# Moving four stores, two weight passes and four sums in a fused attention and MLP kernel

## The chip, the cores and the metric

The kernel runs on one core of a Trainium2 chip. The metric is device time in microseconds (us). The kernel before takes 871.37 us, the median of three runs (870.72, 871.37 and 871.62).

Engines are named as in the profile: PE multiplies matrices (PEld is its loading of weights), DVE is the vector engine, ACT the scalar engine, POOL the third one for element work. SP computes nothing: it issues DMAs, in the order of its queue. ACT and POOL issue some DMAs as well.

## What is computed

Two blocks stand behind each other. The first is attention with a mask: a query sees a key only if six sign bits of their projections agree.

```python
q_bits = (np.einsum('bhsd,dk->bhsk', q, proj) > 0)      # 4 batches, 8 heads, 768 rows, 64 columns
k_bits = (np.einsum('bhsd,dk->bhsk', k, proj) > 0)
...
mask = q_bucket[:, :, :, None] == k_bucket[:, :, None, :]
scores = np.where(mask, scale * np.matmul(q, k.transpose(0, 1, 3, 2)), -1000000000.0)
attn = softmax(scores)
attn_out = np.matmul(attn, v)
```

The second is an MLP on the heads put side by side, `x` of 3072 rows and 512 columns:

```python
h = x @ w_in                                            # 512 x 2048
g = np.maximum(h, 0.0) + alpha * np.minimum(h, 0.0)
out = g @ w_out                                         # 2048 x 512
```

All of it is float32.

## The kernel before

**Attention** (lines 1190 to 1256) is a loop over 16 pairs of heads, `pi`. For each pair PE makes twelve cells of scores (L782, six blocks of keys by two halves of the queries; the key block is the outer index). A cell lies in one of three buffers of PSUM, which the hash of the next pair (L732) and the totals of a pair (L828) use as well, in turn; ACT takes the exponential of the cell (L785) and sets the buffer free. Then PE hashes the next pair (L732), multiplies the exponentials with `v` (`attend`, L815) and sums them (`totals`, L828). DVE adds the exponentials up for the totals (`add_first` L793 to `add_total` L804), turns the totals out of PSUM (L842), and from them makes the factors that the result is multiplied with (L843 to L860). POOL copies pieces of these factors between partitions in four small copies (L851, L852), which the turn at L854 waits for. The result `x` of a pair is stored to the scratch tensor `x_s` in memory by SP (L861).

The sign bits of the next pair come out of ACT as the tile `hr` (L736) and go to the tiles `kb` and `qb` by eight small DMAs (L743): two by ACT's queue, six by POOL's. Each covers one head and one half of the columns. The first cell needs half 0 of `kb` and `qb`, the second needs half 1 of `qb`; half 1 of `kb` is first needed by the seventh.

**Preparing the weights** lies beside attention. `w_in` and `w_out` come as 32 pieces, two for each pair (numbers `i` = 2 `pi` and `i` + 1), loaded by POOL's queue (L590). A piece passes ACT twice (`weight_abs`, L604 and L608) and DVE four times (L614, L620, L645, L648). `weight_abs(i + 2)` and `weight_abs(i + 3)` stand at the end of pair `pi`, ahead of the next pair's exponentials. Four pieces of `w_in` make a group in the tile `wsi`; POOL adds four sums to it (`one`, L667), one each time that `weight_sums` is called, that is, twice a pair. When the four are done, the fifth entry of the list `sums_due` is the function `store`: four DMAs by SP to the scratch tensor `w_in_s` (L672), 448 KB each. The four groups' stores are called in pairs 5, 8, 12 and 15; the last of them in `divide(14)`, which stands in pair 15. `w_out` is stored to `w_out_r` without sums (L659).

**The MLP** multiplies with a scheme of seven products for eight blocks. It runs after the loop, over 60 steps: in each of the 4 batches eight steps `ff1` with `w_in` (`f_0` to `f_7`) and seven steps `ff2` (`z`). A step `f_n` needs the tile `wi` number n, 896 KB, loaded from `w_in_s` by SP (`load_w`, L891). There are three such buffers. Numbers 0, 1 and 2 are loaded in pairs 9, 11 and 15, the rest as buffers come free. It also needs differences of `x`: the blocks are loaded from `x_s` (`load_x`, L875) in pair 5 (block 0 of a list of four), pair 6 (blocks 2 and 3) and pair 8 (block 1), and `sum_x` (L885) makes four differences on DVE, whole tiles of 128 x 768, in pairs 8, 10, 12 and 14. Block 3 becomes the tile `x5`, block 0 `x0`; the first difference is `x5 - x0`. From L1010 on, POOL loads pieces of `w_out_r` (`wo`) beside the first steps of the MLP, 512 KB each.

**What sets the order.** The framework schedules each engine's queue by itself, except where an instruction goes through `do`: that pins it behind the instruction that the program wrote last for the same engine, pinned or not. All work of PE, DVE, ACT and POOL in the loop is pinned so. On SP the loads of `q`, `k` and `v` and the stores are not pinned; the loads of `x` for the first batch and the first three of `wi` are (`pinned`, L866). What a queue holds is issued in order: an instruction that waits holds back all behind it. At the end of a pair the program writes for SP: `v` of pair `pi + 2`, then `load_w` and `load_x`, then `q` and `k` of pair `pi + 3`, in four DMAs each.

```python
        if pi + 2 < NPAIR:
            load(pi + 2, "v")
        if pi in (9, 11, 15):
            load_w((9, 11, 15).index(pi))
        if pi in (5, 6, 8):
            load_x(0, *{5: (0,), 6: (2, 3), 8: (1,)}[pi])
```

Of the kernel before, what the change touches and what calls it, by code (L numbers as in the profile page):

```python
# [13 lines left out]
ALU = mybir.AluOpType  # L14
# [393 lines left out]
def fast_path(  # L408
# [12 lines left out]
    nc = tc.nc  # L421
    P = 128
    B, H, S, D = q.shape
# [62 lines left out]
    def load(pi, name):  # L486
        b, hp = pairs[pi]
        src = {"q": q, "k": k, "v": v}[name]
        if name == "v":
            t = pool.tile([P, 2, NC * D], F32, name=f"vn{pi}", tag="vn")  # L490
            nc.sync.dma_start(t, src[b, 2 * hp : 2 * hp + 2].rearrange("h (p c) d -> p h (c d)", c=NC))
            nat[name, pi] = t
        elif pi and name in BY_BLOCKS:
            load_blocks(pi, name)
        else:
            load_part(pi, name, slice(0, NC), nc.sync)
# [102 lines left out]
    def weight_abs(i, engine=None):  # L599
        i = order[i]  # L600
        lo, hi = halves(i)
        wx[i] = pool.tile([P, 512], F32, name=f"wx{i}", tag="wx")
        wr[i] = pool.tile([P, 512], I32, name=f"wr{i}", tag="wr")
        do(ACT.activation(wr[i], lo, AF.Copy, scale=2.0 ** -29))  # L604
        if engine is DVE:
            do(DVE.tensor_scalar(wx[i].bitcast(U32), hi, 0x7FFFFFFF, None, op0=ALU.bitwise_and))
            return
        do(ACT.activation(wx[i], hi.bitcast(F32), AF.Abs))  # L608
# [39 lines left out]
        do(DVE.tensor_tensor(dst.bitcast(I32), x, r, op=ALU.add))  # L648
        return (dst if i < HW else dst[:, 0])[:, :1]

    sums_due = []

    def weight_group(i):

        i = order[i]
        if i >= HW:
            n, m = divmod(i - HW, 2)
            if m == 1:
                nc.sync.dma_start(w_out_r[:, :, n].rearrange("m p d -> p m d"), wst[HW + n])  # L659
            return  # L660
        n, m = divmod(i, 4)
        if m < 3:
            return
        w = wst[n]

        def one(to, a, op, c):
            do(POOL.tensor_tensor(w[:, to], w[:, a], w[:, c], op=op))  # L667

        def store():
            c, kk = divmod(n, 2)  # L670
            for ii in range(4):
                nc.sync.dma_start(w_in_s[4 * c + ii][:, :, kk], w[:, :, ii])  # L672


        for x in ((3, 5, 2), (5, 0, 5), (4, 3, 0), (6, 1, 4)):
            sums_due.append((one, (x[0], x[1], ALU.subtract, x[2])))
        sums_due.append((store, ()))

    late_sum = const.tile([P, 1], F32, name="late_sum")

# [45 lines left out]
    def hash_bits(pi):  # L726

        ps = two_banks(f"hs{pi}")[:, 0, :CW]
        for half in range(2):
            for n, name in enumerate("kq"):  # L730
                c = D * n + 32 * half
                do(PE.matmul(  # L732
                    ps[c : c + 32], wh2, tr[name, pi][:, half * CW : (half + 1) * CW], start=True, stop=True,
                ))
        raw = pool.tile([P, CW], BF16, name=f"hr{pi}", tag="hr", bufs=1)
        do(ACT.activation(raw, ps, AF.Sign, bias=hb2))  # L736
        bits["q", pi], bits["k", pi] = qbs[pi % 2], kb
        for half in range(2):
            for n, name in enumerate("kq"):
                for s in range(2):  # L740
                    c = D * n + 32 * half + NB * s
                    queue = nc.gpsimd if half or name == "q" else nc.scalar
                    queue.dma_start(  # L743
                        bits[name, pi][D * s : D * s + 2 * NB, half * CW : (half + 1) * CW], raw[c : c + 2 * NB],
                    )

    def hash_first(half):

# [25 lines left out]
    def scores(pi, cells):  # L774
        for kc, g in cells:
            sc = two_banks(f"sc{pi}_{kc}_{g}")
            ks = slice(kc * P, (kc + 1) * P)
            qs = slice(g * CW, (g + 1) * CW)
            for what, first in ((bits, True), (tr, False)):
                for s in range(2):  # L780
                    r = slice(D * s, D * s + D)
                    do(PE.matmul(  # L782
                        sc[:, s, :CW], what["k", pi][r, ks], what["q", pi][r, qs], start=first, stop=not first,
                    ))
            do(ACT.activation(pts[kc][:, g, :, :CW], sc[:, :, :CW], AF.Exp, scale=SCALE / DOWN))  # L785
# [46 lines left out]
    def divide(pi, between=lambda: None):  # L832

        b, hp = pairs[pi]
        n = CW // 32
        a = pool.tile([P, CW], F32, name=f"st{pi}", tag="st", bufs=1)
        r = pool.tile([P, n], F32, name=f"rc{pi}", tag="rc")
        rr = pool.tile([P, NCH, n], F32, name=f"rr{pi}", tag="rr")  # L840
        d = pool.tile([P, NCH, CW], F32, name=f"dn{pi}", tag="dn", bufs=1)
        do(DVE.transpose(a, sums[pi][:, 0, :CW]))  # L842
        do(DVE.tensor_scalar(r, a.rearrange("p (n w) -> p n w", w=32)[:, :, 0], S * EPS, None, op0=ALU.add))  # L843
        for g in range(NCH):
            do(DVE.reciprocal(rr[:, g], r))
        vsum[pi] = pool.tile([P, 1], F32, name=f"vs{pi}", tag="vs")
        do(DVE.tensor_scalar(vsum[pi], av[pi][:, 0, CW : CW + 1], EPS, None, op0=ALU.mult))
        weight_sums(1, vsum[pi])
        for q0 in (0, D):
            q1 = q0 + 32  # L850
            do(POOL.tensor_copy(rr[q0 : q0 + 32, 1], rr[q1 : q1 + 32, 1]))  # L851
            do(POOL.tensor_copy(rr[q1 : q1 + 32, 0], rr[q0 : q0 + 32, 0]))  # L852
        between()
        do(DVE.transpose(  # L854
            d.rearrange("p g w -> p (g w)"),
            rr.rearrange("p g n -> p (g n)").unsqueeze(2).to_broadcast([P, NCH * n, 32]),
        ))

        x = mid.tile([P, NCH, CW], F32, name=f"x{pi}", tag="x", bufs=1)
        do(DVE.scalar_tensor_tensor(x, av[pi][:, :, :CW], vsum[pi], d, op0=ALU.add, op1=ALU.mult))  # L860
        nc.sync.dma_start(x_s[b, hp], x.rearrange("p g w -> p (g w)"))  # L861
# [15 lines left out]
            ))  # L877
            x_m[b, m] = t

    def sum_x(b, n, engine):  # L880

        to, a, c = ((3, 5, 0), (5, 2, 5), (4, 2, 3), (6, 4, 1))[n]
        if to != 5:
            x_m[b, to] = mid.tile([P, 2, CW], F32, name=f"x{b}_{to}", tag=f"x{to}", bufs=1)
        do(engine.tensor_tensor(x_m[b, to], x_m[b, a], x_m[b, c], op=ALU.subtract))  # L885

    def load_w(n):

# [301 lines left out]
    for pi in range(NPAIR):  # L1190
        i = 2 * pi

        def weight_begin():
            if pi == 1:
                turn_blocks(2, "q")
            if pi + 1 < NPAIR:
                turn_blocks(pi + 1, "k")
            weight_clamp(i)
            weight_parts(i)
            add_first(pi)  # L1200

        if pi:
            scores(pi, CELLS)
            divide(pi - 1, weight_begin)
        else:
            rest = [c for c in CELLS if c not in ahead]
            scores(pi, rest[:4])
            weight_abs(0, DVE)
            scores(pi, rest[4:])
            add_first(pi)  # L1210
            weight_clamp(0)
            weight_parts(0)
        if pi in (8, 10, 12, 14):
            sum_x(0, (8, 10, 12, 14).index(pi), DVE)
        weight_sum(i)
        weight_group(i)
        load_weight(i + 3)
        if pi == 0:
            weight_abs(1, DVE)
        weight_clamp(i + 1)  # L1220
        add_third(pi)
        add_last(pi)
        add_total(pi)
        weight_parts(i + 1)
        weight_sums(1, weight_sum(i + 1))
        weight_group(i + 1)
        load_weight(i + 4)
        if pi + 1 < NPAIR:
            hash_bits(pi + 1)
            do(ACT.activation(tr["q", pi + 1], tr["q", pi + 1], AF.Copy, scale=DOWN))  # L1230
        if 0 < pi < NPAIR - 2:
            turn_blocks(pi + 2, "q")
        attend(pi)
        if pi + 1 == NPAIR:
            now = ff1(0, 0)
            now.step(1)
        totals(pi)
        if pi + 1 == NPAIR:
            now.step(5)
            divide(pi)  # L1240
        else:
            weight_abs(i + 2)
        if pi + 2 < NPAIR:
            load(pi + 2, "v")
        if pi in (9, 11, 15):
            load_w((9, 11, 15).index(pi))
        if pi in (5, 6, 8):
            load_x(0, *{5: (0,), 6: (2, 3), 8: (1,)}[pi])
        if pi == 1:
            setup_alpha()  # L1250
        for name in "qk":
            magnitude(pi, name)
            if pi + 3 < NPAIR:
                load(pi + 3, name)
        if pi + 1 < NPAIR:
            weight_abs(i + 3)


# [95 lines left out]
```

## Time and profile before

| | |
|---|---|
| median of three runs | 871.37 us |
| profiled execution | 872.62 us |
| its span, first to last instruction | 870.8 us |
| PE busy | 860.5 us (99%) |
| DVE, ACT, POOL busy | 734.2, 375.0, 119.1 us |
| granted clock of PE, mean | 0.998 |
| memory read, written | 104.87, 28.31 MB |
| first cell of pair 1, of pair 15 | 29.0, 297.6 us |
| first product of the MLP, end of its last | 315.8, 864.1 us |

The profile is that of one execution. Its page gives busy times of the engines, the costliest groups of instructions and the DMAs. Other views of the same trace give the waits (who waited for whom), the instructions in order of time, and the busy time, granted clock and memory traffic of any stretch. In the timeline a row is start, duration, engine, line, operation, output<-input, and in brackets the idle time of the engine ahead of it and what ended it. Rows of SP are the issues of DMAs, not their transfers: how long the data takes is read from the traffic of a stretch.

### The profile page before, as it was taken

To read this page: it belongs to the slowest core of one execution; us is meant where nothing else is said; L and a number is where in the kernel's file an instruction comes from. 1 tells how busy PE (TensorE), PEld (TensorE's weight loads), DVE (VectorE), ACT (ScalarE), POOL (GpSimd) and SP (SyncE) were. 2 spreads that over 40 slices of the span, in tenths; PEclk is the share of its full clock that TensorE was granted. 3 is DMA by queue.
4 is the path that set the end of the run, shared out by engine and by line. 5 is a ranking of instruction groups with operands and counts; after the bars stand their busy time and mean duration, and the time that the engine had idled before them with its cause. 6 is when DMAs were issued, how large, how long until landed. Compare 5 with 4: busy or idle time off the path is not lost.

```text
span 870.8 us, 14641 instructions
## 1 busy us (share of the span) xinstructions
PE 860.5 (99%) x5458; PEld 575.5 (66%) x5458; DVE 734.2 (84%) x1188; ACT 375.0 (43%) x682; POOL 119.1 (14%) x253
## 2 busy tenths in 40 slices
PE   9999999999999999999999999999999999999996
PEld 4444444444445445569985559996558997557996
DVE  6999989999999987899887669897659898568886
ACT  6787878868778733331113331112332112332111
POOL 1322423333435310210000000000000000000001
PEclk9999999999999999999999999999999999999999
DMA  8956796998697446785334335333425433420242
GB/s 197 188 135 130 185 248 176 184 228 207 130 259 177 144 132 236 257 285 222 115 115 121 133 126 165 121 145 92 166 95 163 145 109 115 164 84 1 97 151 72
DMA packets 171104, 135.35 MB, mean 155 GB/s; under 512 B 126240, under 2 KB 155088, under 8 KB 167440
## 3 DMA queue, kind: packets, MB, share of 16 engines
q1 hardware_dynamic: 158528, 108.44, 44.2%
q0 software_dynamic: 9488, 24.56, 9.3%
q10 hardware_dynamic: 3008, 1.33, 0.6%
q8 instruction: 45, 0.74, 0.3%
q14 instruction: 35, 0.29, 0.1%
HBM read 104.87 MB, written 28.31 MB: 153 GB/s over the span
## 4 chain that ended last, share of the span: by engine, by line


## 5 line engine op out<-in xcount | busy, mean ns | idle before, releaser
L782 PE MATMUL sc<-qT,kT 64*128 64x384 f32 x768 | 155.7, 483 | 0.0
L785 ACT ACTIVATE pt<-sc 128x768 f32<-128x768 f32 x192 | 151.5, 811 | 1.2 <-PE sc L782 1.2
L815 PE MATMUL av<-pt,vn 128*32 128x385 f32 (+1 forms) x1536 | 127.0, 485 | 0.0
L815 PEld LDWEIGHTS av<-pt,vn 128*32 128x32 f32 x1536 | 50.3, 109 | 73.8 <-issue 69.8
L782 PEld LDWEIGHTS sc<-qT,kT 64*128 64x128 f32 x768 | 69.2, 187 | 35.0 <-issue 34.0
L975 DVE TENSOR_TENSOR g<-g,g 128x384 f32<-128x384 f32 x128 | 68.3, 554 | 2.2
L1094 POOL DMA_DIRECT2D out_dram<-o x4 | 2.2, 555 | 474.3 <-DVE o L1087 474.3
L782 PE MATMUL sc<-qb,kb 64*128 64x384 bf16 x384 | 65.3, 323 | 1.4 <-ACT pt L785 0.7
L971 DVE SCALAR_TENSOR_TENSOR g<-h,alpha 128x384 f32<-128x384 f32 x60 | 36.8, 614 | 25.2 <-ACT h L964 25.1
L1032 DVE TENSOR_TENSOR ws<-wl 128x512 f32<-128x512 f32 x56 | 38.4, 686 | 21.9 <-DMA wl<-w_out_s 18.0
L1040 DVE TENSOR_TENSOR gs<-g,gs 128x768 f32<-128x768 f32 x56 | 53.3, 952 | 1.0
L1040 DVE TENSOR_TENSOR gs<-g 128x768 f32<-128x768 f32 x56 | 53.2, 950 | 0.0
L782 PEld LDWEIGHTS <-kb 64*128 64x128 bf16 x384 | 21.8, 94 | 36.9 <-issue 13.2
L604 ACT ACTIVATE wr<-raw 128x512 int32<-128x512 uint32 x32 | 22.1, 691 | 35.9 <-DVE wsi L648 18.4
L793 DVE TENSOR_TENSOR accp<-pt,pt 128x1536 f32<-128x1536 f32 x16 | 28.1, 1759 | 8.4 <-ACT pt L785 8.4
L743 POOL DMA_DIRECT2D qb<-hr x60 | 30.1, 507 | 22.8 <-ACT hr L736 22.8
L798 DVE TENSOR_TENSOR accd<-accd,pt 128x1536 f32<-128x1536 f32 x16 | 28.1, 1759 | 1.7
L804 DVE TENSOR_TENSOR accd<-accd,accp 128x1536 f32<-128x1536 f32 x16 | 28.1, 1758 | 0.6
L801 DVE TENSOR_TENSOR accp<-accp,pt 128x1536 f32<-128x1536 f32 x16 | 28.0, 1753 | 0.0
L797 DVE TENSOR_TENSOR accd<-pt,pt 128x1536 f32<-128x1536 f32 x16 | 28.0, 1750 | 0.0
L1230 ACT ACTIVATE qT<-qT 128x768 f32<-128x768 f32 x15 | 12.7, 844 | 26.5 <-DMA kb<-hr 16.4
L915 PE MATMUL f_0a<-x,wi 128*128 128x384 f32 x64 | 23.5, 490 | 0.0
(366 smaller groups left out, 1767.7 us busy)
## 6 DMA issues: line engine op xcount, KB each, us to landing
wi<-w_in_s SPq DMA_DIRECT2D x32, 896.0 KB
wl<-w_out_s SPq DMA_DIRECT2D x16, 1024.0 KB
wl<-w_out_r SPq DMA_DIRECT2D x12, 1024.0 KB
raw<-in_moe_w_in_dram POOLq DMA_DIRECT2D x15, 512.0 KB, 5.2
raw<-in_moe_w_out_dram POOLq DMA_DIRECT2D x14, 512.0 KB, 4.9
w_in_s<-wsi SPq DMA_DIRECT2D x16, 448.0 KB
qn<-in_q_dram SPq DMA_DIRECT2D x64, 96.0 KB
vn<-in_v_dram SPq DMA_DIRECT2D x16, 384.0 KB
```

The costliest lines, as they stand in the source:

```text
L743: queue.dma_start(bits[name, pi][D * s : D * s + 2 * NB, half * CW : (half + 1) * CW], raw[c : c + 2 * NB],)
L782: do(PE.matmul(sc[:, s, :CW], what["k", pi][r, ks], what["q", pi][r, qs], start=first, stop=not first,))
L785: do(ACT.activation(pts[kc][:, g, :, :CW], sc[:, :, :CW], AF.Exp, scale=SCALE / DOWN))
L793: do(DVE.tensor_tensor(accp[pi], p(0), p(1), op=ALU.add))
L797: do(DVE.tensor_tensor(accd[pi], p(3), p(4), op=ALU.add))
L798: do(DVE.tensor_tensor(accd[pi], accd[pi], p(5), op=ALU.add))
L804: do(DVE.tensor_tensor(accd[pi], accd[pi], accp[pi], op=ALU.add))
L815: do(PE.matmul(av[pi][D * s + t : D * s + t + 32, g, :w], nat["v", pi][:, s, kc * D + t : kc * D + t + 32], pts[kc][:, g, s, :w], start=(k ...
L971: do(DVE.scalar_tensor_tensor(new_g(b, m)[:, i], h, al, h, op0=ALU.mult, op1=ALU.max))
L975: do(DVE.tensor_tensor(new_g(b, to)[:, i], g_m[b, x][:, i], g_m[b, y][:, i], op=ALU.subtract))
L1032: do(DVE.tensor_tensor(t, w2[b, n, x], w2[b, n, y], op=op))
L1040: do(DVE.tensor_tensor(t, g2[b, n, x], g2[b, n, y], op=ALU.subtract))
```

## The change

Five things are changed.

- The load of `v` is pinned in SP's queue (for pairs from 2 on), and the stores of `w_in`'s groups are pinned too. They are no longer written where `weight_sums` comes to them: that only puts them on the list `stores_due`, and they are written at the end of the pair, behind the load of `v` and ahead of `load_w`, `load_x` and the loads of `q` and `k`. In pair 15 there is no load of `v` any more; what the program wrote last for SP there is the store of pair 15's `x` (L861, in `divide(15)`).
- `sum_x` makes one half of a difference (128 x 384) in each of the pairs 7 to 14, in place of a whole one in every second pair.
- `weight_abs(3)`, which stood at the end of pair 0, stands behind the first three cells of pair 1.
- POOL issues the bits of `q`'s half 1 ahead of those of `k`'s half 1.
- `weight_abs(i + 3)` at the end of a pair is left out in pair 0 accordingly.

```diff
-            nc.sync.dma_start(t, src[b, 2 * hp : 2 * hp + 2].rearrange("h (p c) d -> p h (c d)", c=NC))
+            ins = nc.sync.dma_start(t, src[b, 2 * hp : 2 * hp + 2].rearrange("h (p c) d -> p h (c d)", c=NC))
+            if pi > 1:
+                do(ins)
...
-    sums_due = []
+    sums_due, stores_due = [], []
...
             for ii in range(4):
-                nc.sync.dma_start(w_in_s[4 * c + ii][:, :, kk], w[:, :, ii])
+                do(nc.sync.dma_start(w_in_s[4 * c + ii][:, :, kk], w[:, :, ii]))
...
-        sums_due.append((store, ()))
+        sums_due.append((stores_due.append, (store,)))
...
-        for half in range(2):
-            for n, name in enumerate("kq"):
-                for s in range(2):
-                    c = D * n + 32 * half + NB * s
-                    queue = nc.gpsimd if half or name == "q" else nc.scalar
+        for name, half, queue in (("k", 0, nc.scalar), ("q", 0, nc.gpsimd), ("q", 1, nc.gpsimd), ("k", 1, nc.gpsimd)):
+            for s in range(2):
+                c = D * "kq".index(name) + 32 * half + NB * s
...
-    def sum_x(b, n, engine):
+    def sum_x(b, n, engine, k=slice(0, 2)):
...
-        do(engine.tensor_tensor(x_m[b, to], x_m[b, a], x_m[b, c], op=ALU.subtract))
+        do(engine.tensor_tensor(x_m[b, to][:, k], x_m[b, a][:, k], x_m[b, c][:, k], op=ALU.subtract))
...
-        if pi:
+        if pi == 1:
+            scores(1, CELLS[:3])
+            weight_abs(3)
+            scores(1, CELLS[3:])
+            divide(0, weight_begin)
+        elif pi:
...
-        if pi in (8, 10, 12, 14):
-            sum_x(0, (8, 10, 12, 14).index(pi), DVE)
+        if 7 <= pi < 15:
+            kk = (pi - 7) % 2
+            sum_x(0, (pi - 7) // 2, DVE, slice(kk, kk + 1))
...
             load(pi + 2, "v")
+        while stores_due:
+            stores_due.pop(0)()
         if pi in (9, 11, 15):
...
-        if pi + 1 < NPAIR:
+        if 0 < pi < NPAIR - 1:
             weight_abs(i + 3)
```

## The prediction

> **What bounds the kernel now.** I read the page's busy times first, then PE's own waits, then the instructions in order of time around each place that the change touches, and last the traffic of short stretches.
>
> ```profile
> PE 860.5 (99%) x5458; PEld 575.5 (66%) x5458; DVE 734.2 (84%) x1188; ACT 375.0 (43%) x682; POOL 119.1 (14%) x253
> ```
>
> PE is the bound from end to end: 870.8 - 860.5 leaves 10.3 us, and most of that is the first and last few. So nothing can be won but PE's stalls, and whatever makes PE wait is lost in full. The view of PE's waits shows little:
>
> ```profile
> PE z_4a L915 <- DMA wl<-w_out_r: 0.9, 1, 0.9
> PE sc L782 <- ACT pt L785: 0.7, 2, 0.4
> PE sc L782 <- DVE st L842: 0.4, 2, 0.2
> ```
>
> Ends of matmuls are modelled, so I measured stalls by starts. An undisturbed pair takes 18.98 us from first cell to first cell, its cells 0.807 us each. Starts later than that, by the trace's start times: pair 1's fourth cell 0.54; pair 6's first three 0.61 in all; pair 9's third 0.60, 11's 0.38, 13's 0.38; around pair 14's totals 0.15, and 0.46 in pair 15. Sum 3.1 us: 0.54 for the weight passes, 0.61 for the bits, 1.97 for the sums of x.
>
> ```profile
> 30.00 0.68 ACT L604 ACTIVATE wr<-raw 128x512 int32<-128x512 uint32 x1 [2.15 <-DVE wsi L648]
> 31.98 0.34 PE L782 MATMUL sc<-qb,kb 64*128 64x384 bf16 x2 [0.38 <-ACT pt L785]
> ...
> 124.68 0.24 PEld L782 LDWEIGHTS <-kb 64*128 64x128 bf16 x2 [0.69 <-DMA kb<-hr]
> ...
> 183.80 0.54 DVE L842 STREAM_TRANSPOSE st<-sm 128x384 f32<-128x384 f32 x1
> ```
>
> First two rows: weight 3's passes sit ahead of pair 1's exponentials. Third: the bits come late, after the stores at 114.1. Last: L842, which frees the totals' buffer for the third cell, 1.63 us after pair 9's first cell, where pairs without a sum before them have 0.45 to 0.65.
>
> The MLP's start is where the change meets something new. SP's queue, then all engines:
>
> ```profile
> 300.03 3.90 SPq L672 DMA_DIRECT2D w_in_s<-wsi  x4
> 306.28 0.34 SPq L861 DMA_DIRECT2D x_s<-x  x1
> ...
> 322.31 0.33 SPq L861 DMA_DIRECT2D x_s<-x  x1
> ```
>
> ```profile
> 322.69 14.28 SPq L891 DMA_DIRECT2D wi<-w_in_s  x3
> 323.03 3.06 POOL L1010 DMA_DIRECT2D wo<-w_out_r  x4 [2.81 <-DVE f_0u L967]
> ...
> 333.56 1.16 PEld L915 LDWEIGHTS f_2a<-x,wi 128*128 128x128 f32 x4
> ```
>
> The last group's stores go out at 300.03, in an idle stretch. The load of wi 2 goes out at 322.69 (the row merges it with the next two), four loads of wo beside it, and PE needs wi 2 at 333.6. Traffic, with the stretches chosen to hold the stores alone, wi 2 alone, wo alone, and (last) after PE's end; the columns at the end are granted clock, DMA share and GB/s:
>
> ```profile
> 301.20:307.70 6.50, 6.50 (x50) 3.89 (x47) 5.35 (x7) 6.50 (x9) 0.48 (x2) 1.00 1.02 284
> 324.30:327.10 2.80, 2.80 (x10) 1.62 (x9) 2.23 (x4) 0.46 (x1) 1.79 (x3) 1.00 0.98 316
> 327.20:331.00 3.80, 3.80 (x14) 2.21 (x13) 2.79 (x6) 1.44 (x3) 0.00 (x0) 1.00 1.01 399
> 867.30:870.70 3.40, 0.00 (x0) 0.00 (x0) 0.00 (x0) 0.00 (x0) 0.00 (x0) 0.50 0.06 17
> ```
>
> In each of the first three the DMA engines are full (0.98 to 1.02).
>
> **The change, part by part.** Differences are against the profiled execution (872.62, 1.25 above the median) and are added to the median, 871.37, since a stall costs the same in both.
>
> *Last group's stores, pair 15: +5.0.* They are written behind the store of pair 15's x, so they leave SP from 322.7 on, 3.9 us of issuing, and wi 2, pinned behind them, leaves at 326.6. The data: x_s has the engines until about 324.2; then 4 x 459 KB at 284 GB/s is 6.5 us, 4 x 524 KB of wo at 399 is 5.3, and 917 KB of wi 2 at 316 is 2.9. All three: 324.2 + 14.7 = 338.9 against 333.6 to 333.9, a stall of 5.0. If wo gave way wholly, wi 2 would be there at 333.9: 0.3. If the mixture is slow (the bits behind the stores at 114.1 came 10.6 us after these, and unmixed the data takes 6.5 + 1.2 from issue), 7.9. I take 5.0: between 331.0 and 334.8 wo and wi 3 share the engines at 388 GB/s, so wo gets its part. In the old order the slack was 6.4 us (wi 2's data ends at 327.2).
>
> *The clock after that stall: +1.5.* The granted clock is 1.00 to PE's end at 864.1 and beyond, and 0.50 from 867.3 on, 3.2 us later; at the start PE works from 1.2 us, and its f32 products take 0.85 us up to 7.1 and 0.51 from 9.8. So a wait of 5.0 us may halve the clock, and work at half clock for up to 5.9 us loses up to 2.95. Bounds 0 and 2.95, I take the middle. The largest stall in the trace, 0.95 us at 443.8, left the clock at 1.00. The Trainium skill (TensorE: Matmul & The Clock Gate, Part 1) says that one idle window of about 3.4 us halves the clock and about 3.4 us of work restores it. By it this term is 0 or 1.7, depending on where the windows lie; no run here shows it in mid-kernel.
>
> *Other groups' stores, pairs 5, 8, 12: -0.6.* They move from 114.1, 171.7 and 251.9 to behind v at 125.2, 182.0 and about 260, out of the way of the bits (issued 7.4 to 4.4 us ahead of a pair's first cell). Pair 6's 0.61 goes; pair 9's is set by L842 anyway. What is queued behind them on SP: a block of x in pairs 5 and 8, two DMAs of q, four of k, the next x_s. They come 4 to 6 us later in issue and up to 9 in data; q is turned by DVE 19 us after v's issue, k a pair later. Bounds: -0.6, and 0 if the later q and k traffic delays the next bits as much. I take -0.6: in most pairs k's loads run just ahead of the bits, and these still end 2 to 5 us early. The pin of v costs 0: v was issued there already, and is used 30 us later.
>
> *Bits of q ahead of k's: 0.* One POOL issue pair, 1.0 us, is moved; in undisturbed pairs both land over 2 us early. Without that cover it would be worth up to 0.3 (the second cell of pair 6), counted above.
>
> *Weight 3 behind three exponentials: -0.1.* An undisturbed exponential starts 1.02 us after its cell and takes 0.81; a cell waits for the exponential three before it, so there are 0.58 us of slack. Before: exponentials late by 1.11, stall 0.54. After: two passes, 1.14 us, between third and fourth exponential, which follow at 0.69 apart when late; the fourth starts 1.03 late, the seventh cell stalls 0.46. The stall moves and hardly shrinks. Bounds -0.54 and +0.1.
>
> *Half-sums: +0.2.* A whole sum costs DVE 0.87 us, a half 0.5 (L975's 128x384 row: 0.55 alone, less some overlap). L842 may end 0.4 us later than it does in quiet pairs before PE feels it. A half fits almost. But in pairs where POOL has a group's sum ahead of its four copies (8, 10, 11, 13, 14), a late L842 pushes the third copy into DVE's long addition L793, and L854 waits 0.4 more:
>
> ```profile
> 225.54 1.72 POOL L851 COPY rr<-rr 32x12 f32<-32x12 f32 x1
> ```
>
> That copy takes 0.19 elsewhere, and happens now in 11, 13 and 14. With a half in each pair the copies collide in all five. Stalls by this reckoning: pair 8 0.1, 9 0.63, 11 0.41, 12 0.44, 14 0.45, 15 0.1: 2.1 against 1.97 before. The Trainium skill (SBUF — State Buffer, Who interferes with whom) says that the second of the two engines to issue blocks for the whole instruction, which speaks against spreading; by it the copies cost as the row shows, without it the halves would win 1.5. Bounds -1.9 (none left) and +0.4.
>
> *The first half waits for x5: +1.5.* In pair 7 DVE gets to it at 152.1. Block 3 of x is issued at 147.6, after v and block 2, and the last of the 768 DMA packets of 1,536 bytes that v and the two blocks make ends at 153.5 in the trace. So DVE waits 1.4 to 1.9 us, with all of pair 7's remaining DVE work behind it, and pair 8's L842, over its slack already, hands that to PE. Bounds 0 (less traffic ahead of it, so that it lands 1.4 us earlier) and 3 (the loads that pair 5's stores push back are still in the queue); I take the lower end of what the packets show.
>
> Sum: 5.0 + 1.5 - 0.6 - 0.1 + 0.2 + 1.5 = +7.5, so 871.4 + 7.5 = 878.9.
>
> **Rivals.**
> - *wi 2 comes in time.* For it: 6.5 us of stores against 6.4 of slack is close, if the engines serve SP's queue first. Against: the shared stretch at 331 to 334.8. Then 0.3 instead of 6.5: 872.7.
> - *Faster.* The mechanism is DVE's backlog at L842: if a half costs no more than its slack of 0.4 and the copies escape L793, all 1.97 goes. It decides at 0.4 us; for it, quiet pairs have L842 at 0.45 to 0.65, against it, the collisions. With x5 and wi 2 in time: 871.4 - 2.7 = 868.7.
> - *Worse.* q or the bits also come late behind the stores in pairs 7, 10 or 14, a stall of 0.6 each as in pair 6, or the mixture is slow: 878.9 + 1.8 + 2.9 = 883.6.
> - *The stores go out early all the same,* their data being ready at 300: excluded, the pin is behind L861.
>
> **How the numbers follow.** Main case (875 to 882) 0.72; wi 2 in time (870 to 873) 0.12; faster 0.07; worse (over 882) 0.05; between 873 and 875 0.04. The range 872.0 to 882.0 holds the main case, most of wi 2 in time and what lies between. A change below 0.2% (1.7 us) can't be told from none here. Faster 0.07 (the faster case), same 0.10 (wi 2 in time, nearly all), slower 0.83.
>
> **What would show it.** Right: PE waits for wi at f_2a, some 5 us, with w_in_s's stores issued after 322; a granted clock of 0.50 after it; DVE waits for x at L885 in pair 7; pair 6 starts without a wait for kb. Wrong: f_2a starts on time, wo's transfers behind wi 2's, or L842 in pairs 8 to 15 within 1.0 us of the first cell.

## The result and the profile after

The change makes the kernel slower: 885.11 us, the median of six runs (883.14 to 886.33), against 871.5 for the kernel before (six runs, 870.72 to 871.75). The ratio is 1.0156, with a 95% interval of 1.0143 to 1.0169. The forecast was 878.9 us, with a range of 872.0 to 882.0: the direction is right, the time is outside the range.

The profiled execution of the kernel after took 884.90 us, its span is 883.1. The engines' busy times on its page first:

```profile
PE 862.3 (98%) x5458; PEld 576.9 (65%) x5458; DVE 734.5 (83%) x1192; ACT 373.6 (42%) x682; POOL 122.1 (14%) x253
```

PE is as busy as before to within 1.8 us, in a span that is 12.3 us longer. So PE waits, and its waits say for whom (total us, times, longest):

```profile
PE f_1b L915 <- ACT f_1b L930: 7.9, 1, 7.9
PE sm L828 <- DVE accd L804: 1.8, 1, 1.8
PE sc L782 <- DVE st L842: 1.4, 5, 0.5
...
PE sc L782 <- ACT pt L785: 0.3, 1, 0.3
```

The first is the MLP's start, but at `f_1b`, which needs `wi` 1, not at `f_2a`, the first user of `wi` 2. The second is pair 7. Neither stands in this view of the kernel before.

Starts of matmuls, set against those of an undisturbed pair (18.98 us) and of an MLP without any of these stalls, divide the 12.35 us of span: before pair 1 -0.26, pairs 1 to 15 +2.19, MLP from its first product to its last +10.12, tail +0.30. The MLP's part is 8.05 at `f_1b`, 2.01 at half clock right behind it, and nothing else: the two kernels each lose a further 1.3 to 1.4 at the first `z` steps, in different places.

Here is the MLP's start, from the rows of the kernel after in order of time:

```profile
324.25 0.33 SPq L861 DMA_DIRECT2D x_s<-x  x1
324.67 4.82 SPq L674 DMA_DIRECT2D w_in_s<-wsi  x4
...
329.54 2.60 SPq L891 DMA_DIRECT2D wi<-w_in_s  x2
334.60 0.62 DVE L971 SCALAR_TENSOR_TENSOR g<-f_0u,alpha 128x384 f32<-128x384 f32 x1 [9.85 <-DMA w_in_s<-wsi]
...
335.20 3.05 POOL L1010 DMA_DIRECT2D wo<-w_out_r  x4 [13.04 <-issue]
...
336.26 0.55 DVE L967 TENSOR_TENSOR f_0p<-f_0p,f_0b 128x384 f32<-128x384 f32 x1
...
336.90 0.46 ACT L930 COPY f_1b<-f_1a 128x384 f32<-128x384 f32 x1 [10.72 <-DVE f_0p L967]
...
337.41 2.93 PE L915 MATMUL f_1b<-x,wi 128*128 128x384 f32 x4 [7.88 <-ACT f_1b L930]
```

Read it from below. PE waits for ACT's copy into the bank of `f_1b`. That copy waits until DVE has added `f_0b` out of the same bank (336.26). And DVE stood still for 9.85 us in front of its first write of `g`, until `w_in_s<-wsi` had landed: the stores themselves, not the load behind them. In the kernel before, the same write of `g` and the same copy had no such wait:

```profile
322.95 0.62 DVE L971 SCALAR_TENSOR_TENSOR g<-f_0u,alpha 128x384 f32<-128x384 f32 x1
...
326.34 0.46 ACT L930 COPY f_1b<-f_1a 128x384 f32<-128x384 f32 x1 [2.10 <-PE f_1a L915]
```

`g` does not use what the stores write, and by the addresses of the built kernel its room does not overlap that of the last `wsi`. What they have in common is a border between pools (a pool is a piece of on-chip memory that the framework hands out to tiles): `wsi` lies in the pool of the attention part, which is closed after pair 15, and `g` is the first tile that DVE writes in the pool `late`, which takes the room over. POOL's loads of `wo`, in the same pool, are late too: 335.20, in place of 323.03 before; the profile names nothing that ended their wait. The stores' data shows in the packets: 3584 of 512 bytes, from 326.1 to 333.7.

In the windows of this start (the columns at the end are granted clock, DMA share and GB/s) PE is idle, the clock halves, and work resumes at half clock:

```profile
333.00:334.40 1.40, 0.00 (x0) 0.00 (x0) 0.00 (x0) 0.00 (x0) 0.00 (x0) 1.00 1.02 334
334.50:337.40 2.90, 0.00 (x0) 0.00 (x0) 2.73 (x5) 0.50 (x2) 2.20 (x3) 0.50 0.99 400
337.40:341.20 3.80, 3.79 (x6) 2.19 (x7) 3.05 (x7) 0.84 (x2) 0.85 (x2) 0.50 0.98 312
341.40:343.00 1.60, 1.60 (x7) 0.94 (x6) 0.11 (x1) 0.48 (x1) 0.00 (x0) 1.00 1.02 410
```

At half clock the products of `f_1b` and `f_1c` start 640 ns apart in place of 323. And in pair 7, the second place, DVE waits for block 3 of `x` and hands it on to the totals (rows of the kernel after):

```profile
154.15 0.56 DVE L885 TENSOR_TENSOR x<-x,x 128x384 f32<-128x384 f32 x1 [2.60 <-DMA x<-x_s]
...
163.78 0.85 PE L828 MATMUL sm<-accd,ones 128*32 128x384 f32 x8 [1.83 <-DVE accd L804]
```

### The profile page after: what moved, and what is told of

Read it like the earlier page. It is cut to its first block, busy times and chain, and to the rows that moved or that the text cites. A ratio compares the mean times of both kernels' runs of the same rounds, so it can differ in the third digit from the quotient of the medians.

```text
span 883.1 us, 14642 instructions
## 1 busy us (share of the span) xinstructions
PE 862.3 (98%) x5458; PEld 576.9 (65%) x5458; DVE 734.5 (83%) x1192; ACT 373.6 (42%) x682; POOL 122.1 (14%) x253
## 4 chain that ended last, share of the span: by engine, by line
## 5 line engine op out<-in xcount | busy, mean ns | idle before, releaser
L793 DVE TENSOR_TENSOR accp<-pt,pt 128x1536 f32<-128x1536 f32 x16 | 28.1, 1758 | 7.3 <-ACT pt L785 7.3
```

Of the source, the lines that this page charges most:

```text
L793: do(DVE.tensor_tensor(accp[pi], p(0), p(1), op=ALU.add))
```

## The experiments

Two theories of the MLP's start were set against each other: that of the prediction (PE waits for `wi` 2), and the one that the rows above suggest (DVE's first tile in a pool waits for the last DMAs out of the pool that was closed).

### The last stores put back, all else as after

```diff
-        sums_due.append((stores_due.append, (store,)))
+        if n == 3:
+            def last():
+                for ii in range(4):
+                    nc.sync.dma_start(w_in_s[4 + ii][:, :, 1], w[:, :, ii])
+            sums_due.append((last, ()))
+        else:
+            sums_due.append((stores_due.append, (store,)))
```

> The kernel after, but the last group's four stores are issued where the kernel before has them (about 300), all else as after. Prediction's theory (wi 2 comes late) and rival (the first tile of the MLP that DVE writes waits for the last stores of the closed memory pool to land) both expect the stall of 7.9 us at f_1b and the half clock behind it to go: 885.1 - 8.05 - 2.0 = 875.0 us. What is left against the kernel before, about +3.6, is then the pairs' own: the difference of stalls in pairs 1 to 15 (5.5 against 3.3) and what lies around them. If the pairs were the cause of the MLP's late start, it would stay near 885.

Measured: 875.71 us (875.37 to 877.8), 1.006 times before (1.0043 to 1.0077); the span falls from 883.1 to 873.6. The row that waited 9.85 us has no wait now, and `wo`'s loads leave beside it, with the bracket that they had in the kernel before:

```profile
325.29 0.62 DVE L977 SCALAR_TENSOR_TENSOR g<-f_0u,alpha 128x384 f32<-128x384 f32 x1
325.37 3.06 POOL L1016 DMA_DIRECT2D wo<-w_out_r  x4 [2.81 <-DVE f_0u L973]
```

So the place of these four stores costs about 9.5 us, and the other parts together about 4 by the medians, 2.8 by the spans of the profiled executions. Which theory holds, this run can't tell.

### The last stores alone, in the kernel before

```diff
-        sums_due.append((store, ()))
+        sums_due.append((stores_due.append, (store,)) if n == 3 else (store, ()))
...
+        while stores_due:
+            stores_due.pop(0)()
         if pi in (9, 11, 15):
             load_w((9, 11, 15).index(pi))
```

(In `store`, `do` pins the DMAs of group 3 alone.)

> The kernel before, with only the last group's four stores moved and pinned as in after. Both theories: the whole loss at the MLP's start, 8.05 + 2.0 us, comes from this step alone: 871.4 + 10 = 881.4 us, with the same wait at f_1b. If it needs the other steps as well (the pairs' shifted loads), it stays well below 881.

Measured: 881.88 us (881.14 to 882.83), 1.0123 times before (1.0106 to 1.014). The same stall stands at the same place, 7.97 at `f_1b` by the starts, and 2.15 at half clock. The step needs no help from the others.

```profile
PE f_1b L917 <- ACT f_1b L932: 7.8, 1, 7.8
```

### `wi` 2 ahead of the last stores

```diff
-        while stores_due:
+        while stores_due and pi < 15:
             stores_due.pop(0)()
         if pi in (9, 11, 15):
             load_w((9, 11, 15).index(pi))
+        while stores_due:
+            stores_due.pop(0)()
```

> The kernel after, but in pair 15 the load of wi 2 is written ahead of the last group's stores. Theory of the prediction (PE waits for wi 2): wi 2 lands by about 330, the stall at the MLP's start is gone, about 875 us. Rival (DVE's first tile of the MLP waits for the last stores to land): the stores land about 2.9 us (the data of wi 2) later, the stall at f_1b stays and grows to some 10 to 11 us, with 2 to 3 us lost to the half clock, about 888 us.

Measured: 886.26 us. PE's longest wait, and DVE's row at the start:

```profile
PE f_1b L915 <- ACT f_1b L930: 9.6, 1, 9.6
```

```profile
337.22 0.62 DVE L971 SCALAR_TENSOR_TENSOR g<-f_0u,alpha 128x384 f32<-128x384 f32 x1 [11.60 <-DMA w_in_s<-wsi]
```

The stall stays and is 1.7 us longer, a little less than the forecast 2 to 3. `f_2a` now follows without a wait, so `wi` 2 was in time and can't be what held PE: the prediction's theory falls as the cause of this stall.

### `wsi` in a pool that stays open

```diff
-                wst[n] = pool.tile([P, NM, 4, P], F32, name=f"wsi{n}", tag="wsi")
+                wst[n] = (mid if n % 2 else pool).tile([P, NM, 4, P], F32, name=f"wsi{n}", tag="wsi", bufs=1)
```

(`mid` is a pool that stays open to the end. The later buffers named in the expectation lose one copy each.)

> The kernel after, but the tile wsi of groups 1 and 3 lies in a pool that is never closed, so that the MLP's first tiles do not take over the memory pool that the last stores read from; some buffers of the MLP's later part (ws3, ws4, gs3, gs4, m, o) are reduced by one to make room, so only the start of the MLP is to be compared. Rival: DVE's first g no longer waits for w_in_s<-wsi, f_1b starts on time; what is left is the wait for wi 2 itself at f_2a, which the packets of after put at 338 against 335.8 needed, 2 to 5 us. Prediction's theory, were it the whole cause: nothing changes at f_1b and the stall stays near 8.

Measured: 884.01 us. DVE and POOL go on at once now, with the stores just issued, and PE waits one step later, for something else. First the rows in order of time, then PE's longest wait:

```profile
325.00 4.78 SPq L674 DMA_DIRECT2D w_in_s<-wsi  x4
325.11 0.62 DVE L971 SCALAR_TENSOR_TENSOR g<-f_0u,alpha 128x384 f32<-128x384 f32 x1
325.28 3.05 POOL L1010 DMA_DIRECT2D wo<-w_out_r  x4 [2.81 <-PE f_0c L915]
...
341.88 2.93 PE L915 MATMUL f_2a<-x,wi 128*128 128x384 f32 x4 [5.59 <-DMA wi<-w_in_s]
```

```profile
PE f_2a L915 <- DMA wi<-w_in_s: 5.6, 1, 5.6
```

At this place only where the tile lies was changed (the buffers that lose a copy belong to later steps), and DVE's wait of 9.85 us is gone, POOL's of 13.04 too: the pool was the cause. What comes up in its place is the stall that was predicted: `f_2a` waits for `wi` 2, 5.6 us (5.75 by the starts) where 5.0 was worked out. The packets show why: `wo`'s 4,096-byte packets run from 328 to 336 beside the stores' 512-byte ones, which end at 338.8 in place of 333.7, and `wi` 2 comes after them. In the kernel after this stall was hidden: PE came to `f_2a` 10 us late anyway.

### Both of these together

> The kernel after with both: wsi of groups 1 and 3 in a pool that is not closed, and in pair 15 the load of wi 2 ahead of the last stores. If the pool's wait and wi 2's late arrival are all that holds up the MLP's start, neither stall is there, the clock stays at 1.00, and the time is that of the kernel with the last stores early, 875.5, plus up to 1 for the buffers taken from the later part. If a third thing holds it (the bare traffic), a stall of some us stays at f_1b or f_2a.

The edit is that of the last two runs together. Measured: 876.61 us. From the MLP's first product to its last it takes 546.14 us, exactly as in the undisturbed runs below, with the last stores as late as in the kernel after, and PE's waits there are gone. The longest that is left, 2.8 us, is in pair 7:

```profile
PE sm L828 <- DVE accd L804: 3.7, 2, 2.8
```

Two things hold up the MLP's start, one behind the other, and there is no third. The total is not 875.5, though the MLP up to its last product takes 1.5 us less than in the run with the last stores early: pair 7, with DVE's wait for `x`, costs 3.7 us in this run in place of 2.4 (see the clock, at the end), and the end of the kernel, where buffers were taken away, takes 1.3 more.

### Two of the four stores

```diff
-            for ii in range(4):
+            for ii in iis:
...
+        if n == 3:
+            sums_due.append((store, (range(2),)))
+            sums_due.append((stores_due.append, (lambda: store((2, 3)),)))
```

> The kernel before with only the last two of the last group's four stores moved to where after has them. Four moved stores held DVE to 333.0, 7.8 us of stall; a store's 459 KB takes 1.6 us at 284 GB/s, so two should release it at 329.7 to 330, and f_1b waits 4.5 to 4.8 us. The clock is the open part: in the runs with stalls of 5.6 to 9.6 us it fell 4.1 to 5.1 us after PE's last product, in those with 2.0 to 2.5 us not at all. With a stall of 4.5: 871.3 + 4.5 = 875.8 without a fall, 877.5 to 878.8 with one.

Measured: 880.26 us. DVE is released at 329.62 and PE waits 4.8 us, as forecast from the stores' data: the wait follows the bytes still under way.

```profile
PE f_1b L921 <- ACT f_1b L936: 4.8, 1, 4.8
```

The clock falls too. Against the profiled execution of the kernel before, the span is 7.72 longer: 4.96 for the stall (by starts), 1.80 at half clock, and 0.95 more lost at the first `z` steps. The forecast with a fall, 877.5 to 878.8, was counted from the median and left the `z` steps out.

### The other parts one at a time

These four were read from their traces; the kernel before, run once beside them, took 874.19, which is 2.7 above its median, so nothing is concluded from their times (871.37, 874.39, 871.27 and 870.70 us). Stalls are by starts of cells against an undisturbed pair.

*Block 3 of `x` a pair earlier, in the first run's kernel:*

```diff
-            load_x(0, *{5: (0,), 6: (2, 3), 8: (1,)}[pi])
+            load_x(0, *{5: (0, 3), 6: (2,), 8: (1,)}[pi])
```

> The kernel of the run before with the last stores early, and block 3 of x (the tile x5) loaded in pair 5 in place of pair 6. If DVE's wait for x5 in pair 7 costs what the trace of after shows, PE's stall of 2.03 us there goes, and pair 8's L842 comes on time or up to 0.4 late in place of 0.65: the span falls by 2.0 to 2.5 us, from 873.6 to about 871.4. Rival: the load takes PE's other inputs' place in the queue of pair 5, and a stall of that size comes up in pair 6.

The half-sum of pair 7 starts at 152.00 without a wait, pair 7 loses 0.13 in place of 2.39, pair 8 nothing in place of 0.65, and the pairs' stalls together fall by 2.79. The span is 869.6. No stall comes up in pair 6. The span falls by more than the 2.0 to 2.5 expected because the first `z` steps lose 1.5 less in this run as well.

*The halves alone, in the kernel before:*

> The kernel before with the sums of x in eight halves as in after, and nothing else. By the prediction's two terms (first half waits for x5, +1.5; collisions of POOL's copies, +0.2) and by after's trace (pair 7 2.0, then 0.65, 0.40, 0.41, 0.42, 0.42, 0.22 in place of 1.97) the span grows by 2.0 to 2.6 us, to about 873. If the wait for x5 came from the stores that were pushed behind v, it is gone here, and the span stays within 0.7 of before's 870.8.

Pair 7 loses 2.47, pair 8 0.65, pairs 9, 11, 12 and 14 0.41 to 0.43 each. The span is 872.6, 1.85 above that of the kernel before and just under the range expected: from pair 1 to the MLP's first product it takes 3.2 us more, but the first `z` steps lose 1.3 less. The stores behind `v` are not what makes block 3 late, since they are not there in this run. Its first half-sum:

```profile
155.35 0.56 DVE L885 TENSOR_TENSOR x<-x,x 128x384 f32<-128x384 f32 x1 [3.03 <-DMA x<-x_s]
```

*Weight 3's passes alone, in the kernel before:*

> The kernel before with weight 3's two passes behind the third exponential of pair 1, and nothing else. Prediction: the stall moves from the fourth cell (0.54) to the seventh (0.46), -0.1. After's trace: pair 2 begins with a stall of 0.29 more, since DVE ends pair 1 later; if that belongs to this move, the sum is +0.2, if it belongs to another part of the change, it is not there.

Pair 1's stall moves to the seventh cell (0.49), and pair 2 starts 0.30 late: 0.96 in the two pairs against 0.72 before, so +0.24. The rows at pair 2's start show the new wait: the copy of `alpha` out of PSUM, which DVE reaches only at 49.58, and behind it the second cell.

```profile
48.66 0.34 PE L782 MATMUL sc<-qb,kb 64*128 64x384 bf16 x2
...
49.58 0.13 DVE L560 COPY alpha<-alps 128x16 f32<-128x16 f32 x1
...
49.77 0.34 PE L782 MATMUL sc<-qb,kb 64*128 64x384 bf16 x2
```

*The first three groups' stores alone, in the kernel before:*

> The kernel before with the stores of the first three groups behind the pinned load of v, as in after, and nothing else; the last group's stores and the order of the bits stay as before. Prediction: pair 6's first cells lose their wait for the bits, -0.6, and nothing else moves: span 870.2. If the order of the bits' DMAs was what took the wait away in after, 0.3 of it stays.

The stalls of pairs 5 and 6 (0.10 and 0.52) are both zero, with the old order of the bits. So the stores are what took that wait away, and the order of the bits' DMAs is worth nothing that shows. (The span is 868.9, under the 870.2 expected; here too the first `z` steps lose 1.3 less than in the kernel before, as they do in the two runs ahead of this one, which have the old stores.)

### A version that is faster than both

It keeps the part that gained, leaves the last stores where they were, and puts the halves where DVE has idle time: ahead of L793, which in undisturbed pairs of the kernel before (2 to 5, 7, 8 and 10) waits 0.58 to 0.72 us for an exponential. Its row in pair 7 there:

```profile
148.50 1.76 DVE L793 TENSOR_TENSOR accp<-pt,pt 128x1536 f32<-128x1536 f32 x1 [0.58 <-ACT pt L785]
```

```diff
             weight_parts(i)
+            if pi > 7:
+                sum_x(0, (pi - 8) // 2, DVE, slice(pi % 2, pi % 2 + 1))
             add_first(pi)
```

> A version meant to be faster than both: the kernel before, the first three groups' stores behind the pinned load of v (worth 0.8 us in the run that did that alone), the last group's stores where before has them, and the sums of x as halves in pairs 8 to 15, each written just ahead of DVE's addition L793, which waits 0.58 to 1.08 us for an exponential in undisturbed pairs. If a half of 0.5 us fits in that idle time, the stalls of pairs 9, 11, 13, 14, 15 (0.39, 0.39, 0.40, 0.15, 0.45) go: 871.3 - 0.8 - 1.8 = 868.7 us. Rival: the half ends after the exponential does, or POOL's copies collide with L793 all the same, and half of it stays: 869.6.

Measured: 869.36 us against 871.81, ratio 0.9973 (0.9964 to 0.9982), a gain of 2.45 us where 2.6 was expected. Of the stalls of pairs 9 to 15 one of 0.12 is left, in pair 12; pair 1's stays. The half fills the gap ahead of the addition (rows of DVE in pair 9; the lines have moved by four):

```profile
182.72 0.54 DVE L846 STREAM_TRANSPOSE st<-sm 128x384 f32<-128x384 f32 x1
...
185.33 0.43 DVE L622 TENSOR_SCALAR wx<-wx 128x512 uint32<-128x512 uint32 x1
185.67 0.55 DVE L889 TENSOR_TENSOR x<-x,x 128x384 f32<-128x384 f32 x1
186.14 1.76 DVE L797 TENSOR_TENSOR accp<-pt,pt 128x1536 f32<-128x1536 f32 x1
```

With weight 3's two passes taken apart as well:

```diff
             scores(pi, CELLS)
+            if pi == 1:
+                weight_abs(3, parts="r")
             divide(pi - 1, weight_begin)
...
-            weight_abs(i + 3)
+            weight_abs(i + 3, parts="rx" if pi else "x")
```

> The run before this one, and weight 3's two passes on ACT apart: the one that DVE needs first stays at the end of pair 0, the other follows the twelfth exponential of pair 1. One pass of 0.57 ahead of the exponentials is within the 0.58 us that the cells have to spare, so pair 1's stall of 0.54 at the fourth cell goes: 868.2 us. If the bits of the next pair come late behind the second pass, or DVE does, pair 2 begins with a stall, and it is the same as the run before.

Measured: 869.07 us, ratio 0.997 (0.9959 to 0.9982): the same as the run before it. Pair 1's stall falls from 0.71 to 0.16, and pair 2 starts 0.46 late, at the copy of `alpha` again. DVE has hardly a gap in pair 1; when PE waits less, it catches up with DVE.

## Why the prediction was wrong

The table has the terms of the sum as put and as measured; the last column says where.

| Step | put | measured | from |
|---|---|---|---|
| last group's stores, pair 15 | +5.0, at `f_2a` | +8.05, at `f_1b` | after |
| the clock after that stall | +1.5 | +2.01 | after |
| other groups' stores | -0.6 | -0.61 (pairs 5 and 6) | first three groups alone |
| bits of `q` ahead of `k`'s | 0 | 0 | the same run |
| weight 3 | -0.1 | +0.24 | weight 3 alone |
| half-sums | +0.2 | 0.0 (pairs 7 to 15: 2.02 against 2.01) | block 3 earlier |
| first half waits for x5 | +1.5 | +2.7 (2.03 in pair 7, 0.65 in pair 8) | after |
| sum | +7.5 | +12.4 | spans: +12.35 |

**The step that failed is the first, "a stall of 5.0".** Its working asked only when `wi` 2 would land, and took DVE and POOL to be free. It followed the stores as something that is in the way of a load, and not as readers of a tile whose room is handed on: the first tile written in `late` waits for them. With `wsi` in another pool this wait went. As an account of `wi` 2 the step was good, as the run with `wsi` in the open pool shows: 5.6 us at `f_2a`, near its 5.0. But two waits that overlap are paid once, at the later end, and the longer one had not been seen. Its readings had two slips beside this: `wi` 2's last packet in the kernel before ends at 328.3, not at 327.2, so the slack was 5.3 us and not 6.4, and by its own terms `wi` 2 would be there at 333.6, not at 333.9, if `wo` gave way. The rival "worse", with 7.9 for a slow mixture of transfers, was near the size by the wrong way: in the kernel after there was hardly any mixture, since `wo` was held up as well.

**The clock** was right as a mechanism and 0.5 short: 1.5 was the middle of its bounds, 0 to 2.95, which hold 2.01. It was measured behind another stall than the one it was put for; behind the wait for `wi` 2 alone it was 2.7.

**x5** was right in place and mis-sized. DVE waits 2.60 where 1.4 to 1.9 was read from the packets, and the working stopped at PE's stall in pair 7: DVE catches up only in part, and pair 8's L842 starts 1.67 us after its first cell, another 0.65. Taking the load forward removes both.

**Weight 3** has the wrong sign. The stall moved as worked out (0.46 at the seventh cell), but DVE's chain through pair 1 moved with it, and pair 2's `alpha` was not looked at.

**Half-sums** and the **other groups' stores** came out near what was put, the collisions of POOL's copies included (they take 1.70 to 1.76 us in the pairs 8, 10, 11, 13 and 14 that were named). The stalls that follow are 0.40, 0.41, 0.42, 0.42 and 0.22 in pairs 9, 11, 12, 14 and 15 of the kernel after, where 0.63, 0.41, 0.44, 0.45 and 0.1 had been worked out.

The medians lie 13.6 apart and the spans 12.35; the profiled execution of before was 1.25 above the median of its first three runs. Its loss of 1.30 at the first `z` steps, which nine of the other traces don't have, is of that size; that it is the reason is not shown.

## What to carry to other kernels

When a DMA out of a tile is moved to a later time, ask two questions: which transfers it now stands in front of, and who is given the tile's room next. Here the closing of a pool made its last DMAs a gate for the first tiles of the next one, for DVE and POOL alike; a tile that is still being stored at such a border belongs in a pool that stays open, or its store ahead of it. That alone won only 1 us here (884.0 against 885.1), since the next wait stood right behind; only with the transfers put in order as well was the start free.

A small piece of work costs nothing where its engine waits for another anyway, and up to its length where the engine's lateness is handed on: the same eight halves cost 2.0 us of stalls behind L793 and 0.1 ahead of it.

## What was not expected of the hardware

The clock falls after less idle time than the prediction allowed, and in steps. The edges are worked out from the mean granted clock of half-microsecond windows, idle time from the end of PE's last product to the next start:

| Run | PE idle | at half clock | that is | lost at half clock |
|---|---|---|---|---|
| both together, pair 7 | 162.4 to 165.2 (2.8) | 164.8 to 168.2 | 3.4 | not separated |
| two of four stores | 327.6 to 332.4 (4.8) | 333.0 to 336.4 | 3.4 | 1.8 |
| `wsi` in the open pool | 336.3 to 341.9 (5.6) | 340.4 to 347.2 | 6.8 | 2.7 |
| last stores alone | 328.0 to 335.8 (7.8) | 333.2 to 340.0 | 6.8 | 2.15 |
| after | 329.5 to 337.4 (7.9) | 334.5 to 341.3 | 6.8 | 2.0 |
| `wi` 2 first | 330.4 to 340.0 (9.6) | 334.4 to 344.7 | 10.2 | 2.4 |

Idle times of 1.8 to 2.3 us in pair 7 (the kernel after, the halves alone) left the clock at 1.00. In the run with two stores it fell half a microsecond after work had resumed, and in the first row a wait of 2.8 us was enough:

```profile
163.90:165.40 1.50, 0.21 (x4) 0.23 (x8) 1.48 (x2) 0.00 (x0) 0.00 (x0) 0.78 0.96 283
165.50:168.00 2.50, 2.50 (x14) 0.79 (x8) 2.47 (x4) 1.13 (x2) 1.55 (x3) 0.50 1.17 165
```

The times at half clock are one, two and three times 3.4 us. That agrees with the Trainium skill (TensorE: Matmul & The Clock Gate, Part 1), which says that activity is judged over windows of about 3.4 us that run on regardless of the program. The traces show such windows: in each run the changes of the clock lie whole multiples of 3.41 us apart (in the kernel after at 6.78, 334.46, 341.29 and 880.59: 96, 2 and 158 windows). What such a window must be, they show more closely than the page's "idle window": the one before the fall in pair 7 (161.3 to 164.8) was idle for 2.4 of its 3.4 us only, so a window that is idle for the most part counts. In all traces together, windows at full clock with up to 1.9 us of idle time left it at 1.00, and those with 2.25 us or more were followed by half clock. By an estimate from these two figures, a gap of some 2 to 4 us halves the clock or not by where it lies in the windows: 2.3 us (the halves alone) did not, 2.8 did. And 1.7 us, half of one window, is not the most that a stall costs behind it: work that resumes inside a window gets the full clock only at the end of the next (with `wsi` in the open pool, 1.9 us of work in the window 340.4 to 343.8 did not bring it back), which is why up to 2.7 us were lost, and no more after 9.6 us of idle time than after 5.6.
